# A weight's sign bit from a parametric relu on ScalarE instead of Abs and an instruction on VectorE

## The chip, the cores and the metric

One core of a Trainium2 chip runs the whole program. The metric is the device time of one launch in microseconds (us). Five engines work side by side, each with an in-order queue of its own: TensorE (PE; its weight loads are listed as PEld), VectorE (DVE), ScalarE (ACT), GpSimd (POOL) and SyncE (SP), which here issues all DMA transfers of tensors.

## The reference

An attention in two steps over 8 batches, 8 heads, 576 tokens and 64 features per head, followed by a Fourier mixing over tokens and features, a normalization without learned weights and a feed-forward part:

```
def sm_attn(qq, kk, vv):
    s = scale * np.matmul(qq, kk.transpose(0, 1, 3, 2))
    a = softmax(s)
    return np.matmul(a, vv)
p_packed = sm_attn(p, k, v)                 # 32 packed tokens per head
x = heads side by side of sm_attn(q, p_packed, p_packed)   # [8, 576, 512]
u = x + real(fft(fft(x, axis=1), axis=2))
un = (u - mean(u)) / sqrt(var(u) + 1e-6)
out = u + maximum(un @ w_ch1, 0) @ w_ch2    # w_ch1 [512, 2048], w_ch2 [2048, 512]
```

`w_ch1` and `w_ch2` come as 64-bit floats (a numpy scalar division made them so), everything else as 32-bit floats.

## The kernel before, in words

The 8 x 576 rows of `u` are worked in nine tiles of 512 rows. `front(b)` computes a batch's attention and Fourier mixing into rows of `u`; `ffn` runs the feed-forward part of one tile, and lets the `front` of the next batch advance a piece at a time in between. Only the front of batch 0 runs ahead of the first tile.

`ffn` goes over 16 blocks j of 128 hidden units. For each, `up(j)` (matmuls L648) multiplies the tile with a block of `w1` into PSUM tile `ph`, ScalarE takes the relu into `hh` (L654), VectorE subtracts that from the exact value into `hl` (L655), and `down(j - 1)` (matmuls L665) multiplies `hh` and `hl` of the block before with a block of `w2` into the accumulators `acc`. The PSUM tile `ph` is a single buffer, so the next `up` waits until `hl` has read it. To keep float32 accuracy each operand is split in two parts, and three matmuls are done for one. For the weights that split is `wsplits`: ScalarE rounds a block into `wr_h` (L99), GpSimd subtracts into `wr_l` (L100); it is done again in every tile, from `w1f` and `w2f`, which hold all weights in SBUF as 32-bit floats. At the end of a tile VectorE adds the result to `u` (L701), and a DMA writes it out.

The change is in `load_weights(j)`, which turns block j of both weights from 64-bit into 32-bit floats. This is done once, for 16 blocks x 2 weights = 32 blocks of 128 x 512. A 64-bit float is seen as two 32-bit words, `low` and `high`. Its fields are 1 sign bit, 11 exponent bits with a bias of 1023, 52 mantissa bits; a 32-bit float has 1, 8 (bias 127) and 23. The word `high` is read as if it were a 32-bit float: then the upper 8 of the 11 exponent bits stand in its exponent field. Multiplying by `REBIAS = 2.0 ** -112` takes 112 x 8 = 896 = 1023 - 127 off the 11-bit exponent. Abs clears the sign. Now a shift to the left by 3 (L179) puts exponent and 20 mantissa bits in place; L180 shifts the three missing mantissa bits in from `low`; L181 puts the sign bit back in from `high`. L179 to L181 are on VectorE, the Abs (L178) on ScalarE.

`fetch` (L166) brings a block of 64-bit words into a staging place, from SyncE's queue. The first six blocks go into parts of `w1f` and `w2f` that are not yet in use; from then on three places rotate, two buffers `wst` and one piece of `ubuf`. A fetch into a place waits until the last instruction that read it is done; before the change that is L181 of the block that stood there.

The order in which each engine works is set in two ways. From the second tile on it is the order of the program text (`manual_schedule`). Ahead of that, in the front of batch 0 and in all of the first tile, a planner lists the instructions of all engines by estimated costs and dependencies; all 32 blocks are converted in that part. Inside the first tile, the program text places `load_weights(j + 2)` in every second step, of which there are two in a block j.

Of the kernel before, what the change touches and what calls it, by code (L numbers as in the profile page):

```python
# [9 lines left out]
F32 = mybir.dt.float32  # L10
F32R = mybir.dt.float32r
I32 = mybir.dt.int32
AF = mybir.ActivationFunctionType
ALU = mybir.AluOpType
# [39 lines left out]
REBIAS = 2.0 ** -112  # L54
# [23 lines left out]
def tile_kernel(ctx, tc, kpT, qT, v, w1, w2, tabC, tabS, tabR, tabB, tabT, sel, ident_d, out):  # L78
    nc = tc.nc
# [78 lines left out]
    def fetch(j, n):  # L158
        i = stages.pop(0)
        if i is None:  # L160
            st = work.tile([P, 512, 2], I32, tag="wst", name="wst", bufs=2)
        elif i < 0:
            st = spot(n, i, [P, 512, 2]).bitcast(I32)
        else:
            st = ubuf[:, i:i + 2, :].rearrange("p a n -> p (a n)").bitcast(I32).rearrange("p (n t) -> p n t", t=2)
        nc.sync.dma_start(st, (w1, w2)[n][:, j, :].bitcast(I32).rearrange("p (n t) -> p n t", t=2))  # L166
        fetched[j, n] = st

    def load_weights(j):

        for n, dst in enumerate((w1f, w2f)):
            if (j, n) not in fetched:
                fetch(j, n)
            st = fetched.pop((j, n))
            low, high = st[:, :, 0], st[:, :, 1]
            c = dst[:, j, :].bitcast(I32)

            nc.scalar.activation(c.bitcast(F32), high.bitcast(F32), AF.Abs, scale=REBIAS)  # L178
            nc.vector.tensor_scalar(c, c, 3, None, ALU.logical_shift_left)  # L179
            nc.vector.scalar_tensor_tensor(c, low, 29, c, ALU.logical_shift_right, ALU.bitwise_or)  # L180
            nc.vector.scalar_tensor_tensor(c, high, -0x80000000, c,  # L181
                                           ALU.bitwise_and, ALU.bitwise_or)

# [540 lines left out]
    for j in range(ORDER[0].count("D"), LEAD):  # L726
        load_weights(j)
# [3 lines left out]
    for t, (first, tk) in enumerate(tiles):  # L731

        gen = front(t + 1) if t + 1 < B else iter(())
        ended = []

        def step(i):

            next_step()
            if t > 0 and i in (0, 2):
                next(rest, None)  # L740
            elif not ended and next(gen, None) == "rest":
                ended.append(gen)
            if t == 0 and i % 2 == 0 and i // 2 + LEAD < NJ:
                load_weights(i // 2 + LEAD)
            assert i < 2 * NJ - 1 or t + 1 >= B or ended

        nxt = Turned(tiles[t + 1][1]) if t + 1 < len(tiles) else None

        with tc.manual_schedule(engines=MANUAL) if t > 0 else nullcontext():
            ffn(first, cur, step, nxt, t + 1 >= B)  # L750
        cur, rest = nxt, gen
# [101 lines left out]
```

## Time and profile before

| | us |
|---|---|
| median of 3 runs (lowest to highest) | 1041.44 (1039.57 to 1041.57) |
| the profiled execution | 1041.16 |
| its span on the core | 1039.4 |

| engine | busy us | share of the span | instructions |
|---|---|---|---|
| PE | 981.9 | 94% | 5692 |
| DVE | 635.6 | 61% | 1296 |
| POOL | 470.1 | 45% | 419 |
| ACT | 425.7 | 41% | 883 |

The span is the time from the first to the last instruction on the core; some 1.8 us of the execution lie around it. A busy share is a mean over the whole span. The page also cuts the span into 40 slices of 26 us, and a table of stretches gives each engine's busy time between any two points of time.

### The profile page before, as it was taken

How to read it: one execution, taken by the hardware profiler on the slowest of the kernel's cores; microseconds unless marked ns; L12 is line 12 of the kernel's file. 1: busy time of each engine (PE TensorE's matmuls, PEld its weight loads, DVE VectorE, ACT ScalarE, POOL GpSimd, SP SyncE). 2: the span in 40 equal slices, each digit the busy share in tenths (PEclk: the TensorE clock that was granted, in tenths of full speed). 3: DMA queues.
4: the chain of work that ended last, by engine and by line, in shares of the span. 5: the costliest groups of instructions: out<-in, count | busy, mean ns of one | idle time of the engine just before them, and what ended most of it. 6: DMA issues, size and time to landing. Idle time of an engine off the chain costs nothing.

```text
span 1039.4 us, 14908 instructions
## 1 busy us (share of the span) xinstructions
PE 981.9 (94%) x5692; PEld 797.1 (77%) x5692; DVE 635.6 (61%) x1296; ACT 425.7 (41%) x883; POOL 470.1 (45%) x419
## 2 busy tenths in 40 slices
PE   6378879999999999999999999999999999999998
PEld 2356658778888788778877887788778888887886
DVE  3898999558655775569465946685658663114112
ACT  2554435344444344444344344344444443323222
POOL 1535544445444543454336534553445444444443
PEclk9699889999999999999999999999999999999999
DMA  9215425130004100310022002200120001001001
GB/s 336 94 57 188 149 81 143 40 118 28 1 1 138 49 1 1 134 52 1 2 92 94 1 1 91 96 1 1 41 97 1 1 2 40 1 1 42 1 1 41
DMA packets 17742, 58.64 MB, mean 56 GB/s; under 512 B 2081, under 2 KB 2465, under 8 KB 17670
## 3 DMA queue, kind: packets, MB, share of 16 engines
q1 hardware_dynamic: 17670, 57.68, 16.4%
q8 instruction: 45, 0.74, 0.3%
q14 instruction: 27, 0.22, 0.1%
HBM read 48.24 MB, written 9.44 MB: 55 GB/s over the span
## 4 chain that ended last, share of the span: by engine, by line
PE 74%; DVE 16%; ACT 4%; issue 3%; DMA 2%; POOL 2%; SPq 0%; ACTq 0%; DVEq 0%; POOLq 0%
PE ph L648 33%; PE acc L665 30%; DVE ubuf L568 2%; DVE turned L420 1%; PE po L327 1%; DVE w1f L181 1%; DVE w2f L180 1%; DVE hl L655 1%; DMA wst<-w 1%; ACT hh L654 1%; DVE turned L416 1%; ACT junk L218 1%; DVE w2f L181 1%; PE s L270 1%; DVE w1f L180 1%
## 5 line engine op out<-in xcount | busy, mean ns | idle before, releaser
L100 POOL TENSOR_TENSOR wr_l<-w1f,wr_h 128x512 fp32r<-128x512 f32 x144 | 192.3, 1335 | 402.4 <-ACT wr_h L99 402.4
L655 DVE SCALAR_TENSOR_TENSOR hl<-ph,hh 128x512 fp32r<-128x512 f32 x144 | 98.8, 686 | 297.9 <-ACT hh L654 297.8
L648 PE MATMUL ph<-uh,wr_h 128*128 128x512 f32 (+1 forms) x580 | 232.7, 401 | 16.4 <-DVE hl L655 14.5
L100 POOL TENSOR_TENSOR wr_l<-w2f,wr_h 128x512 fp32r<-128x512 f32 x144 | 195.1, 1355 | 90.0 <-ACT wr_h L99 88.6
L665 PE MATMUL acc<-wr_h,hh 128*128 128x512 f32 x576 | 228.0, 396 | 3.3 <-ACT wr_h L99 3.3
L648 PE MATMUL ph<-ul,wr_h 128*128 128x512 f32 (+1 forms) x580 | 230.0, 397 | 0.6 <-DVE ul L100 0.4
L648 PE MATMUL ph<-uh,wr_l 128*128 128x512 f32 (+1 forms) x580 | 230.2, 397 | 0.0
L665 PE MATMUL acc<-wr_l,hh 128*128 128x512 f32 x576 | 227.2, 394 | 3.1 <-POOL wr_l L100 3.1
L665 PE MATMUL acc<-wr_h,hl 128*128 128x512 f32 x576 | 226.1, 393 | 0.0
L654 ACT ACTIVATE hh<-ph 128x512 fp32r<-128x512 f32 x144 | 86.0, 597 | 285.3 <-PE ph L648 285.2
L648 PEld LDWEIGHTS ph<-uh,wr_h 128*128 128x128 f32 x580 | 110.3, 190 | 51.5 <-DVE hl L655 17.9
L648 PEld LDWEIGHTS ph<-uh,wr_l 128*128 128x128 f32 x580 | 110.4, 190 | 25.8 <-issue 1.7
L665 PEld LDWEIGHTS acc<-wr_h,hh 128*128 128x128 f32 x576 | 108.4, 188 | 27.3 <-ACT wr_h L99 3.5
L665 PEld LDWEIGHTS acc<-wr_l,hh 128*128 128x128 f32 x576 | 108.3, 188 | 26.7 <-POOL wr_l L100 5.5
L648 PEld LDWEIGHTS ph<-ul,wr_h 128*128 128x128 f32 x580 | 110.6, 191 | 23.3 <-DVE stat L214 1.1
L665 PEld LDWEIGHTS acc<-wr_h,hl 128*128 128x128 f32 x576 | 108.1, 188 | 23.2
L99 ACT CAST wr_h<-w1f 128x512 fp32r<-128x512 f32 x144 | 88.4, 614 | 11.6 <-DVE w1f L181 6.0
L99 ACT CAST wr_h<-w2f 128x512 fp32r<-128x512 f32 x144 | 89.4, 621 | 8.4 <-PE ph L648 6.9
L218 ACT ACTIVATE junk<-ubuf,stat 128x512 f32<-128x512 f32 x36 | 25.8, 717 | 69.4 <-DVE stat L214 69.4
L609 PE MATMUL untp<-ident,un 128*128 128x128 f32 x144 | 36.9, 272 | 1.6 <-DVE un L602 1.6
L238 PE MATMUL py<-gh,fh 128*128 128x258 f32 x64 | 19.0, 302 | 18.2 <-ACT fh L480 16.6
L100 POOL TENSOR_TENSOR gl<-turned,gh 128x516 fp32r<-128x516 f32 x16 | 24.5, 1532 | 23.4 <-ACT gh L99 22.4
(205 smaller groups left out, 1343.7 us busy)
## 6 DMA issues: line engine op xcount, KB each, us to landing
kp<-kpT SPq DMA_DIRECT2D x16, 608.0 KB, 4.9
out<-ubuf SPq DMA_DIRECT2D x36, 256.0 KB, 2.1
vt<-v SPq DMA_DIRECT2D x14, 640.0 KB, 4.6
wst<-w SPq DMA_DIRECT2D x17, 512.0 KB, 3.7
qt<-qT SPq DMA_DIRECT2D x14, 576.0 KB, 4.6
ubuf<-w SPq DMA_DIRECT2D x9, 512.0 KB, 3.7
w1f<-w SPq DMA_DIRECT2D x3, 512.0 KB, 10.9
w2f<-w SPq DMA_DIRECT2D x3, 512.0 KB, 11.3
```

The source lines that it names most:

```text
L99: nc.scalar.copy(hi, src)
L100: (lo_eng or nc.vector).tensor_tensor(lo, src, hi.bitcast(F32), ALU.subtract)
L180: nc.vector.scalar_tensor_tensor(c, low, 29, c, ALU.logical_shift_right, ALU.bitwise_or)
L181: nc.vector.scalar_tensor_tensor(c, high, -0x80000000, c, ALU.bitwise_and, ALU.bitwise_or)
L218: nc.scalar.activation(junk, u, AF.Square, bias=st[:, 1:2], scale=-1.0, accum_out=st[:, 2:3])
L238: nc.tensor.matmul(o, lh, rh, start=first, stop=False)
L568: nc.vector.scalar_tensor_tensor(u_of[key], qe, sign, pe, ALU.mult, ALU.add, accum_out=stat_of[key][:, 0:1])
L609: nc.tensor.transpose(tp[:, c * P:(c + 1) * P], un[:, c * P:(c + 1) * P], ident)
L648: nc.tensor.matmul(ph[:, t], l[:, c * P:(c + 1) * P], r[:, c, t], start=(k == 0), stop=(k == 11))
L654: nc.scalar.activation(hh[:, :T], ph[:, :T], AF.Relu)
L655: nc.vector.scalar_tensor_tensor(hl[:, :T], ph[:, :T], 0.0, hh[:, :T].bitcast(F32), ALU.max, ALU.subtract)
L665: nc.tensor.matmul(acc[i], l[:, w], r, start=(j == 0 and k == 0), stop=(j == NJ - 1 and k == 2))
```

## The change

ScalarE's Abs is replaced by a parametric relu with the same scale and `alpha = -2.0 ** 32`. A positive value comes out multiplied by 2^-112, as before. A negative one is also multiplied by -2^32: it becomes positive, and its exponent field is 32 larger, that is, bit 28 of the word is set (the rebiased exponent of these weights leaves that bit 0). The shift by 3 that follows takes bit 28 to bit 31, which is the sign bit. L181 is dropped.

```
-            nc.scalar.activation(c.bitcast(F32), high.bitcast(F32), AF.Abs, scale=REBIAS)
+            nc.scalar.activation(c.bitcast(F32), high.bitcast(F32), AF.Prelu, scale=REBIAS, alpha=-2.0 ** 32)
             nc.vector.tensor_scalar(c, c, 3, None, ALU.logical_shift_left)
             nc.vector.scalar_tensor_tensor(c, low, 29, c, ALU.logical_shift_right, ALU.bitwise_or)
-            nc.vector.scalar_tensor_tensor(c, high, -0x80000000, c,
-                                           ALU.bitwise_and, ALU.bitwise_or)
```

With a blank line that the diff adds, the parametric relu is L179 in the changed file, the shift L180 and the instruction with `low` L181; every later line has a number smaller by one (`hl` L654, the last addition L700).

## Rows read from the trace of the kernel before

**Rows 1.** The page, busy times and slices, whole span

```profile
PE 981.9 (94%) x5692; PEld 797.1 (77%) x5692; DVE 635.6 (61%) x1296; ACT 425.7 (41%) x883; POOL 470.1 (45%) x419
...
PE   6378879999999999999999999999999999999998
...
DVE  3898999558655775569465946685658663114112
...
PEclk9699889999999999999999999999999999999999
```

**Rows 2.** Stretches: start:end, length, each engine's busy us, clock, DMA share, GB/s

```profile
69.88:186.45 116.57, 99.96 (x528) 76.33 (x528) 111.05 (x209) 53.73 (x109) 60.77 (x48) 0.91 0.43 131
...
201.00:305.30 104.30, 103.97 (x641) 85.91 (x641) 69.27 (x147) 43.57 (x94) 45.73 (x39) 1.00 0.14 47
```

**Rows 3.** Line L655 to 205 us, who waited for it: us, times

```profile
  PEld ph L648: 17.9, 9
  PE ph L648: 14.5, 8
```

**Rows 4.** Chain of waits in order of time: start, us, what

```profile
68.67 0.60 DVE w1f L181
69.28 0.60 DVE w2f L181
69.88 0.60 DVE hl L655
```

**Rows 5.** Waits of SyncE's DMA queue, 62 to 186.45 us: total, times, longest

```profile
SPq L166 <- DVE w1f L181: 50.7, 12, 9.4
SPq L166 <- DVE w2f L181: 40.6, 11, 8.5
```

**Rows 6.** Line L181, one form: min/median/max ns, first and last start

```profile
L181 DVE SCALAR_TENSOR_TENSOR w1f<-w1f x3: 676/676/681, 54.1 to 74.3; 128x512 int32<-128x512 int32 x3
```

**Rows 7.** Stretches, line L181 alone: VectorE's busy us

```profile
48.07:69.88 21.81, 2.63 (x4) 0.95 0.18 55
69.88:186.45 116.57, 26.89 (x28) 0.91 0.43 131
```

**Rows 8.** VectorE in order of time: start, us, line, operation

```profile
90.56 1.79 DVE L181 SCALAR_TENSOR_TENSOR w1f<-wst,w1f 128x512 int32<-128x512 int32 x1
92.28 1.80 DVE L180 SCALAR_TENSOR_TENSOR w2f<-wst,w2f 128x512 int32<-128x512 int32 x1
```

**Rows 9.** GpSimd in order of time, the same stretch

```profile
90.34 1.47 POOL L100 TENSOR_TENSOR wr_l<-w1f,wr_h 128x512 fp32r<-128x512 f32 x1
91.76 1.77 POOL L100 TENSOR_TENSOR wr_l<-w2f,wr_h 128x512 fp32r<-128x512 f32 x1
```

**Rows 10.** Stretches, matmuls of L648 alone: TensorE's busy us, weight loads

```profile
69.88:186.45 116.57, 45.90 (x156) 32.18 (x156) 0.91 0.43 131
...
201.00:305.30 104.30, 47.67 (x192) 35.48 (x192) 1.00 0.14 47
```

**Rows 11.** Line L178, slowest form (ns) and ScalarE's idle time before it

```profile
L178 ACT ACTIVATE w1f<-w1f x3: 654/687/692, 23.2 to 48.1; 128x512 f32<-128x512 f32 x3
...
  DMA ubuf<-w: 14.5, 7
  DMA wst<-w: 12.4, 6
```

**Rows 12.** Line L179, VectorE's idle time before it: us, times

```profile
  ACT w2f L178: 2.0, 2
  ACT w1f L178: 1.7, 2
```

**Rows 13.** ScalarE's groups, whole span: the table load

```profile
L113 ACT ACT_TABLE_LOAD x1 | 1.3, 1283 | 0.7 <-PEq L845 0.7
```

**Rows 14.** ScalarE in order of time: Exp (L385), then Abs (L178)

```profile
109.33 0.69 ACT L385 ACTIVATE s<-s 128x576 f32<-128x576 f32 x1 [0.64 <-POOL s L382]
...
110.64 0.67 ACT L178 ACTIVATE w2f<-wst 128x512 f32<-128x512 f32 x1
```

## The prediction, made before the changed kernel ran

> **What bounds the kernel now.** I read the page's busy shares and slices first. TensorE is busy 94% of the span, and from the seventh of its 40 slices (156 us) on it shows nines; the slices ahead of that are the only ones in which it has gaps, in which VectorE shows eights and nines, and in which the granted clock shows a six and eights [rows 1]. The changed lines run only there, because the weights are rebuilt once, before and during the first tile of the feed-forward part, and are then kept.
>
> The table of stretches makes this a number. From 69.88 us (the first `hl` done) to 186.45 us (the last rebuilt weight done) VectorE is busy 111.05 of 116.57 us, so idle 5.5 us; TensorE is busy 99.96 and idle 16.6, at a mean granted clock of 0.91, a mixture of the two levels, 2.4 and 1.2 GHz. In a later stretch of 104.30 us TensorE is busy 103.97 at clock 1.00, the upper level throughout, and VectorE only 69.27 [rows 2]. So the first tile is limited by VectorE, the others by TensorE.
>
> Who waits for whom confirms it: TensorE's first matmuls of an `up` step wait for `hl`, VectorE's split of the hidden layer, eight times for 14.5 us, its weight loads 17.9 us [rows 3]. `hl` is short, but stands in VectorE's queue behind weight instructions: in the chain of waits it comes right after two L181 of 0.60 us each [rows 4]. Last, the DMA queue: the fetches of further weights wait 50.7 + 40.6 = 91.3 us, 23 times, and always for L181, which is the last reader of the staging buffer [rows 5]. VectorE therefore sets both TensorE's pace and the pace of the loads.
>
> **The change part by part.** *Removed: 32 times L181.* Alone it takes about 0.68 us [rows 6], but consecutive VectorE instructions overlap, and the chain shows a step of 0.60 [rows 4]. That is the lower bound of what leaves the queue: 32 x 0.60 = 19.2 us. The upper bound is their whole busy time, 2.63 + 26.89 = 29.5 us [rows 7], less the 0.07 of overlap each (0.68 - 0.60; 2.2 us): 27.3 us. The 8.1 us between the bounds are L181 instructions that ran longer, up to 1.79 us. These stretches coincide with GpSimd's `wr_l`: the L181 at 90.56 ran 1.79 us while GpSimd's subtraction ran from 90.34 to 91.81, and the L180 that follows ran 1.80 us beside the next one [rows 8, 9]. GpSimd's work stays, so part of this waiting goes to whatever VectorE does next. I take half of it: 19.2 + 4.05 = 23.3 us out of VectorE's queue.
>
> The Trainium skill bears on that half and speaks against it. Its page "SBUF — State Buffer" (section "SBUF: two separate sides") says that a VectorE instruction with two SBUF inputs and a GpSimd instruction that reads SBUF exclude each other for a whole instruction, the later one blocking. The trace agrees at 90.56 (GpSimd ends at 91.81, L181 0.54 us later). By the rule the wait would pass whole to the next L180, and the sum would be by the lower bound, 19.2.
>
> *What VectorE's relief is worth.* Of the 32, four lie before 69.88, on the chain there, 2.4 us by 0.60 each. The other 28 give 20.9 of the 23.3 us, so VectorE alone would finish the stretch in 116.57 - 20.9 = 95.7 us. What is late next is TensorE. Its 99.96 us contain matmuls at the low clock: L648 takes 45.90/156 = 0.294 us a piece here, 47.67/192 = 0.248 later, so 156 x 0.046 = 7.2 us go if the clock recovers with the gaps [rows 10]; TensorE's floor is 99.96 - 7.2 = 92.8 us. 95.7 stands above the floor by only 2.9, over 13 `up` steps of unequal VectorE load: where a step has little VectorE work, TensorE limits it and the saving is lost. For this I take off 3.3 us, a little over that margin, as an estimate. Gain: 23.3 - 3.3 = 20.0 us. The ends of this term: no loss (gain 23.3), or the largest gain, by the floor, 116.57 - 92.8 = 23.8 and 2.4 ahead of it, 26.2.
>
> *Buffers.* The staging buffer is now free after L180, an instruction earlier; each of the 23 waits of the fetches [rows 5] ends earlier. It is the same relief as above, and no second gain; it keeps the loads ahead.
>
> *Changed: Abs becomes Prelu, 32 times on ScalarE.* The trace of before has no Prelu. Abs takes 0.687 us in its slowest form, with waits of 26.9 us in 13 cases for the weight's DMA [rows 11]. ScalarE is busy in under half of the stretch, 53.73 of 116.57 [rows 2], and VectorE waits for it only four times, 3.7 us [rows 12]. So I take 0. Bounds: nothing gained below 0, since the instruction still reads and writes 128x512; above, one more instruction of the same kind each, 32 x 0.69 = 22 us of ScalarE time, hidden in its 62.8 idle us unless it comes while VectorE waits (four times: 2.8 us).
>
> *Moved.* Nothing in the source; but the first tile's order is not written by hand, the planner orders it over all engines and will do so anew with 32 instructions fewer. The trace can't price that; I widen the range by 3 us on both sides.
>
> *Sum.* The profiled execution took 1041.16 us (span 1039.4). 1041.2 - 20.0 = 1021.2. It lies 0.3 us under the median of the runs, which I neglect: 1021 us. All later tiles only start earlier.
>
> **The rivals.** *The loads bound the stretch.* Then only what is ahead of the stream goes: the seven L181 up to the one that the first of these fetches waits for, 7 x 0.60 = 4.2 us: 1037 us. For it: ScalarE already waits for DMA 13 times [rows 11]. Against: every fetch waits for L181, not for a DMA [rows 5].
>
> *Prelu needs another activation table than Exp.* The trace has one table load, 1.283 us [rows 13]. In ScalarE's order weights and Exp alternate (as at 109.33 and 110.64, [rows 14]) so that 12 loads would come: six into and six out of the weights' function. 12 x 1.28 = 15.4 us, if all on the path: 1021 + 15 = 1036 us. For it: nothing. Against: Abs, Copy, Square and Relu ran beside Exp on that one load. The Trainium skill, "ScalarE: Activation LUTs" (section "Table sets: the hidden batching unit"), names relu and abs among the fillers of Exp's set and does not name Prelu; its switch costs 2.66 us with the drain, by which the sum would be 1021 + 32 = 1053, and the trace shows no drain's price.
>
> *Slower: VectorE runs into its own data.* VectorE's queue is in order. If it reaches L179 before the weight has landed, `hl` waits behind it. Today ScalarE waits 26.9 us for weights and VectorE feels 3.7 of it, being late itself [rows 11, 12]. If all of it came through, 26.9 - 3.7 = 23.2 us: 1021 + 23 = 1044 us. It decides the sign from 20 us on, 0.87 us for each of the 23 streamed weights. Against: a faster VectorE frees the buffers sooner, so the loads start sooner too.
>
> **How the numbers follow.** Forecast 0.77; loads 0.09; table 0.04; slower by VectorE's own data or by a bad new order 0.07; a gain wholly lost in between 0.03. The forecast's own range: 26.2 + 3 gained at the most (1012), 19.2 - 3.3 - 3 at the least (1028), and 2.8 more if Prelu is dear (1031). To leave out no more than 2 in 10 I reach part of the way to the two cases at 1036 and 1037: 1012 to 1033. A run of this kernel can tell about 0.2%, 2.1 us, from no change. Faster: 0.77 + 0.09 + 0.04 = 0.90, less 0.01 for the tails; same 0.04; slower 0.07.
>
> **What would show it.** Right: L181's group gone, VectorE's busy time in the first 190 us down by 20 to 27 us, the first L701 at about 181 instead of 201 us, `up` steps (one `hl` to the next) about 7.4 instead of 9.0 us, TensorE's wait for `hl` cut to a few us, the clock near 1.00, the tiles after it unchanged in length. L180 longer than before would show that the waiting for GpSimd passed on. Wrong: more than one table load; VectorE's idle time before L179 in tens of us; ScalarE's instruction of L178 well over 0.69 us; or a first tile as long as before with TensorE's gaps put down to something else, `wr_h` or the DMA.

## The result and the profile after

The changed kernel takes 1026.9 us in the median (4 runs, 1025.99 to 1027.88) against 1040.56 (4 runs) for the kernel before beside it; the ratio is 0.9876, 95% interval [0.9861, 0.9891]. It is 13.7 us faster; forecast were 20.0, range 1012 to 1033.

The page of the changed kernel, busy times and slices, to be set beside [rows 1]:

```profile
span 1025.3 us, 14876 instructions
...
PE 978.5 (95%) x5692; PEld 795.6 (78%) x5692; DVE 608.8 (59%) x1264; ACT 425.0 (41%) x883; POOL 463.1 (45%) x419
...
PE   6489889999999999999999999999999999999998
...
DVE  3897994559465856677556846594658562114112
...
PEclk9699899999999999999999999999999999999999
```

VectorE has 32 instructions and 26.8 us less to do. ScalarE's busy time is the same within 0.7 us. Where the 14 us come from is seen by cutting the span at the first addition into `u` (L701 before, L700 after), that is, at the end of the first tile. First the kernel before, then the changed one (columns as in [rows 2]):

```profile
0.00:201.10 201.10, 152.75 (x921) 114.58 (x922) 165.75 (x335) 89.73 (x186) 88.64 (x101) 0.91 0.42 135
201.10:1039.40 838.30, 829.17 (x4772) 682.54 (x4771) 469.83 (x963) 335.94 (x697) 381.43 (x319) 1.00 0.11 37
```

```profile
0.00:187.22 187.22, 149.40 (x921) 113.13 (x922) 139.58 (x302) 89.29 (x186) 83.36 (x101) 0.91 0.43 146
187.22:1025.30 838.08, 829.15 (x4772) 682.50 (x4771) 469.26 (x963) 335.69 (x697) 379.70 (x319) 1.00 0.11 37
```

The eight later tiles take 838.3 and 838.1 us: all of the gain, 13.9 us, lies in the first tile and ahead of it. VectorE was relieved of 26.2 us there, and half of that arrived. I cut the first tile at three instructions: the first, sixth and twelfth `hl` and the end. The kernel before, then the changed one:

```profile
69.80:114.86 45.06, 38.49 (x240) 27.48 (x241) 41.25 (x69) 19.93 (x42) 23.32 (x17) 0.89 0.54 172
114.86:170.64 55.78, 47.48 (x225) 37.70 (x224) 54.17 (x112) 25.39 (x51) 27.78 (x22) 0.91 0.36 107
170.64:201.09 30.45, 27.98 (x135) 22.52 (x135) 20.70 (x40) 13.41 (x27) 15.89 (x13) 1.00 0.17 51
```

```profile
66.95:103.91 36.96, 35.77 (x240) 25.89 (x241) 29.29 (x58) 21.10 (x43) 20.97 (x17) 0.95 0.69 232
103.91:159.97 56.06, 46.79 (x227) 37.60 (x227) 51.76 (x109) 26.23 (x51) 26.65 (x23) 0.91 0.38 119
159.97:187.22 27.25, 27.11 (x133) 22.10 (x132) 11.04 (x22) 11.93 (x25) 14.63 (x14) 1.00 0.00 1
```

Ahead of the first `hl` 2.85 us are gained, in the first stretch 8.1, in the last 3.2; the middle one, the longest, takes 0.3 us longer than before. In the first and the last TensorE is now busy nearly throughout (35.77 of 36.96, 27.11 of 27.25), so relieving VectorE further can bring little there. In the middle VectorE is nearly as full as before, 51.76 of 56.06, and TensorE idles 9.3 us. Yet it is in the middle that the change took VectorE instructions away too. What took their place is told by the order: between the sixth and the twelfth `hl` the kernel before has finished 10 conversions of 32 (the 18th to the 27th), the changed one 13 (the 20th to the 32nd, all that are left). The planner moved conversions, and three short instructions that prepare the next tile, forward into the time that the change made free; little is left for VectorE in the last stretch (11.04 of 27.25).

The lines that answer to [rows 3], [rows 5], [rows 11] and [rows 12], from the changed kernel. Who waited for `hl`, line L654, to 190 us:

```profile
  PEld ph L647: 9.8, 4
  PE ph L647: 9.6, 3
```

What the fetches on SyncE's queue waited for:

```profile
SPq L166 <- DVE w1f L181: 32.5, 12, 12.4
SPq L166 <- DVE w2f L181: 32.2, 11, 8.1
```

The parametric relu, line L179, the form that was slowest before:

```profile
L179 ACT ACTIVATE w1f<-w1f x3: 652/681/687, 22.5 to 47.2; 128x512 f32<-128x512 f32 x3
```

VectorE's idle time before the shift, line L180, and ScalarE's table load:

```profile
  ACT w2f L179: 4.3, 5
  ACT w1f L179: 2.7, 5
```

```profile
L113 ACT ACT_TABLE_LOAD x1 | 1.3, 1283 | 0.7 <-PEq L844 0.7
```

TensorE still waits 9.6 us for `hl`, in only three waits. The longest, 4.40 us, ends at 116.15. ScalarE's half of that step, `hh`, was done at 112.00, but `hl` stood in VectorE's queue behind three conversion instructions and two short transposes (start, us, instruction):

```profile
110.24 1.65 DVE L181 SCALAR_TENSOR_TENSOR w2f<-wst,w2f 128x512 int32<-128x512 int32 x1
111.81 1.49 DVE L180 TENSOR_SCALAR w1f<-w1f 128x512 int32<-128x512 int32 x1
113.23 1.48 DVE L180 TENSOR_SCALAR w2f<-w2f 128x512 int32<-128x512 int32 x1
...
115.45 0.64 DVE L654 SCALAR_TENSOR_TENSOR hl<-ph,hh 128x512 fp32r<-128x512 f32 x1
```

Each of the two shifts took some 1.5 us there, against 0.43 in the median; GpSimd was at work beside them, from 111.30 to 114.42.

The parametric relu takes what Abs took, on the same one table load.

### The profile page after: what moved, and what is told of

Its sections match the earlier page's. It is cut to its first block, busy times and chain, and to the rows that moved or that the text cites. A ratio compares the mean times of both kernels' runs of the same rounds, so it can differ in the third digit from the quotient of the medians.

```text
span 1025.3 us, 14876 instructions
## 1 busy us (share of the span) xinstructions
PE 978.5 (95%) x5692; PEld 795.6 (78%) x5692; DVE 608.8 (59%) x1264; ACT 425.0 (41%) x883; POOL 463.1 (45%) x419
## 4 chain that ended last, share of the span: by engine, by line
PE 76%; DVE 11%; ACT 5%; DMA 3%; issue 2%; POOL 2%; ACTq 0%; SPq 0%; DVEq 0%; POOLq 0%
PE ph L647 35%; PE acc L664 30%; DVE ubuf L567 2%; DMA wst<-w 2%; DVE turned L419 1%; ACT hh L653 1%; PE po L326 1%; PE s L269 1%; ACT junk L217 1%; DVE turned L415 1%; POOL wr_l L100 1%; PE e1tp L303 1%; DVE hl L654 1%; ACT wr_h L99 1%; DVE w2f L181 1%
## 5 line engine op out<-in xcount | busy, mean ns | idle before, releaser
L654 DVE SCALAR_TENSOR_TENSOR hl<-ph,hh 128x512 fp32r<-128x512 f32 x144 | 98.8, 686 | 305.3 <-ACT hh L653 305.0
L100 POOL TENSOR_TENSOR wr_l<-w2f,wr_h 128x512 fp32r<-128x512 f32 x144 | 192.4, 1336 | 91.9 <-ACT wr_h L99 91.9
L664 PEld LDWEIGHTS acc<-wr_l,hh 128*128 128x128 f32 x576 | 108.2, 188 | 26.8 <-POOL wr_l L100 5.4
L567 DVE SCALAR_TENSOR_TENSOR ubuf<-qe,pe 128x512 f32<-128x512 f32 x32 | 34.6, 1115 | 0.5
```

What stands on the lines that cost most here:

```text
L100: (lo_eng or nc.vector).tensor_tensor(lo, src, hi.bitcast(F32), ALU.subtract)
L567: nc.vector.scalar_tensor_tensor(u_of[key], qe, sign, pe, ALU.mult, ALU.add, accum_out=stat_of[key][:, 0:1])
L654: nc.vector.scalar_tensor_tensor(hl[:, :T], ph[:, :T], 0.0, hh[:, :T].bitcast(F32), ALU.max, ALU.subtract)
L664: nc.tensor.matmul(acc[i], l[:, w], r, start=(j == 0 and k == 0), stop=(j == NJ - 1 and k == 2))
```

## The experiments

Times are medians; beside each stands the ratio to the kernel before, run beside it on the same chip.

**Which of the two edits it is.** e1 is the changed kernel with Abs back, e2 the kernel before with the parametric relu:

```
e1  -  AF.Prelu, scale=REBIAS, alpha=-2.0 ** 32      +  AF.Abs, scale=REBIAS
e2  -  AF.Abs, scale=REBIAS                          +  AF.Prelu, scale=REBIAS, alpha=-2.0 ** 32
```

> The changed kernel with Abs put back in place of the parametric relu, the VectorE instruction still dropped; the weights lose their sign, so that part of the computation is wrong. Every engine has the same instruction order as the changed kernel. Theory (the gain is VectorE's relief, the kind of activation costs nothing): within 1.5 us of the changed kernel's 1026.9. Rival (the parametric relu itself is slower or faster than Abs on the path): off by more than 3 us, 32 instructions by 0.1 us or more.

> The kernel before with the parametric relu in place of Abs, and the VectorE instruction kept (it sets a sign bit that is already set). Instruction order as in the kernel before. Theory: within 1.5 us of the kernel before, 1040.6, for it is the VectorE instruction that counts. Rival (parametric relu matters): off by more than 3 us.

e1: 1027.67 us, 0.9884 [0.9869, 0.9899]; e2: 1039.35 us, 0.9998 [0.9985, 1.0011]. The whole gain is the dropped VectorE instruction's; the kind of activation costs nothing, and the rival of a dear or cheap parametric relu falls. In the first tile e2 has the instruction order of before and e1 that of the changed kernel, so their traces also repeat the cut of the first tile. The middle stretch of e2 and of e1:

```profile
113.92:169.28 55.36, 45.83 (x220) 36.22 (x221) 53.98 (x111) 24.73 (x49) 27.56 (x22) 0.94 0.36 108
```

```profile
103.50:159.81 56.31, 46.27 (x225) 36.92 (x226) 52.15 (x108) 25.96 (x51) 25.93 (x23) 0.94 0.38 119
```

Again the middle is no shorter with the instruction dropped.

**Is it VectorE's relief, or the luck of a new order?** In e3 (changed) and e4 (before) the compute engines follow the program text in the first tile too:

```
-        with tc.manual_schedule(engines=MANUAL) if t > 0 else nullcontext():
+        with tc.manual_schedule(engines=MANUAL):
```

> The changed kernel with the first tile's compute engines in the order of the program text instead of the planner's, so that two weights are converted for each hl and none ahead of need. Theory A (VectorE's relief was spent by the planner on conversions far ahead of need, and hl and with it TensorE came late): faster than the changed kernel, 1014 to 1022 us. Theory B (what limits the changed kernel's first tile is the arrival of the weights): no faster, 1027 us or more, with VectorE idle before the shift for the conversion's activation well above the 7.0 us of the changed kernel.

> The kernel before with the first tile in the order of the program text. Theory A: VectorE is full in nearly all steps there, in any order, so little moves: 1033 to 1042 us, and the distance to the changed kernel in the same order is larger than 13.7 us, 16 to 24. Rival D (the gain of the change was the luck of a new planner's order, not VectorE's relief): the two kernels in the order of the text lie within 6 us of each other.

e3: 1035.39 us, 0.9959 [0.9943, 0.9975]; e4: 1050.56 us, 1.0105 [1.0089, 1.0121]. With the first tile in the order of the text (the front of batch 0 ahead of it is still the planner's) the change is worth 15.2 us, so luck (rival D) falls. All three numbers of theory A missed, the 15.2 too, for which it said 16 to 24: the order of the text makes the changed kernel 8.5 us slower and the kernel before 10.5. It does bring two conversions for each `hl`, but TensorE's order is fixed with it, and it stands for 7.7 us in front of the front's matmuls, in e3 (`who waited <- for whom: total, times, longest`):

```profile
PE py L237 <- ACT fh L479: 7.7, 1, 7.7
```

So e3 says nothing on theory A; it needs an order changed in one place. The time fits theory B, but B's sign is missing: VectorE's idle time before the shift is 8.2 us, hardly more than the 7.0 of the changed kernel.

**Conversions held back.** One ordering edge on VectorE, in e5 for all blocks with k = 2, in e6 with k = 3:

```
-            nc.vector.tensor_scalar(c, c, 3, None, ALU.logical_shift_left)
+            sh = nc.vector.tensor_scalar(c, c, 3, None, ALU.logical_shift_left)
+            if j - k in hl_of:          # hl_of[j]: the hl of block j
+                tc.add_manual_dep(sh.ins, hl_of[j - k], NoSync, ...)
```

> The changed kernel with one ordering edge added on VectorE: the shift of block j's weights stands behind hl of block j - 2, so that conversions can't run further ahead of need than two blocks; the planner orders all else. Theory A (in the changed kernel the planner spends VectorE's relief on conversions ahead of need, in the middle of the first tile, while TensorE waits for hl): 1017 to 1024 us. Rival A2 (in the middle it is the front's own work that fills VectorE, the conversions are not what holds hl up): 1025 us or more, with TensorE's wait for hl as long as in the changed kernel, 9.6 us.

> The same with the edge to hl of block j - 3, one block looser. Theory A: between the changed kernel (1026.9) and the tighter edge, 1019 to 1026 us. Rival A2: within 1.5 us of the changed kernel.

e5: 1025.21 us, 0.9852 [0.983, 0.9873]; e6: 1027.69 us, 0.9878 [0.9857, 0.99]. In the medians e5 is 1.7 us faster than the changed kernel, and 1.2 outside theory A's range; the intervals of the two ratios overlap. e6 is no faster. Held back from the start, the conversions leave the first stretch, where there is room, for the middle and the last. 12 still lie in the middle, against 13, but they are spaced: two for each `hl`, where the changed kernel has 1, 3, 1, 0, 5 and 3. And the middle of e5 is 4.2 us shorter than the changed kernel's:

```profile
105.55:157.39 51.84, 43.39 (x222) 34.90 (x221) 47.46 (x106) 26.87 (x52) 25.80 (x23) 0.97 0.45 135
```

So in the middle the edge did in part what theory A said: TensorE waits 6.2 us for `hl` there instead of 8.1 (A2 said as long as before). The larger part is that its own work takes 43.39 us instead of 46.79, with 222 matmuls instead of 227 and at clock 0.97 instead of 0.91. In the total little of it shows, for in this execution the first `hl` came only at 70.39 us. In the changed kernel it came at 66.95 and in e1 at 66.04, although the compute engines have the same order in all three up to there; why is open. The 2.85 us that I counted ahead of the first `hl` are smaller than this difference between single traces, so they are not shown to come from the change.

**The price of one VectorE instruction in every conversion.** e7 drops the instruction with `low` as well, e8 does the sign instruction of the kernel before twice:

```
e7  -            nc.vector.scalar_tensor_tensor(c, low, 29, c, ALU.logical_shift_right, ALU.bitwise_or)
e8  +            nc.vector.scalar_tensor_tensor(c, high, -0x80000000, c,
    +                                           ALU.bitwise_and, ALU.bitwise_or)
```

> The changed kernel without the VectorE instruction that puts the three lowest mantissa bits in either, so 32 instructions of the same kind fewer again; the weights lose their last three bits. If VectorE still limits the middle of the first tile: 5 to 10 us faster than the changed kernel, 1017 to 1022 us, less than the first 32 gave since TensorE has only some 11 idle us left there. If the arrival of the weights is the limit (theory B): less than 3 us faster.

> The kernel before with the sign instruction done twice, 32 VectorE instructions more. If VectorE limits the whole first tile before the change, each costs its full place in the queue, 0.60 to 0.85 us: 1060 to 1067 us, and so the gain of the change was less than the price because something else took over after it. If one such instruction is worth 0.43 us in general (13.7 / 32, the planner fitting the rest into gaps): 1054 us.

e7: 1022.76 us, 0.9827 [0.9804, 0.985]; e8: 1054.03 us, 1.0135 [1.0106, 1.0163]. From four VectorE instructions a conversion to one, the steps in the medians are 13.1, 13.7 and 4.1 us, where 32 instructions of at least 0.60 us are 19.2. So even from e8 to the kernel before, with VectorE fuller still, only 0.41 us each arrive, which is what the second of e8's two views said. e7's 4.1 us lie between the 5 to 10 that I expected and the 3 of theory B. The two kernels were not timed side by side, and by the ratios to the kernel before the step is 5.1, so the time alone doesn't decide between the two. The trace does: all weights are converted by 112.1 us, so from there on their arrival can't be the limit. e7's three stretches:

```profile
69.98:103.75 33.77, 33.75 (x240) 25.60 (x241) 19.26 (x48) 22.90 (x47) 16.84 (x15) 1.00 0.87 293
103.75:154.22 50.47, 43.02 (x219) 34.49 (x218) 38.05 (x87) 19.93 (x41) 24.21 (x23) 0.97 0.11 35
154.22:183.01 28.79, 28.79 (x142) 23.83 (x141) 9.90 (x23) 12.14 (x25) 14.73 (x14) 1.00 0.00 1
```

In the first stretch TensorE has no gap left (33.75 of 33.77). In the middle only three conversions are left, VectorE idles 12.4 us, and the stretch still takes 50.5 us. The 5.6 us gained there are partly lost again: the first `hl` comes 3.0 us later than in the changed kernel, and the last stretch is 1.5 us longer. The chain of waits shows what the middle consists of (start, us, what):

```profile
112.98 0.69 DVE hl L653
113.67 0.64 DVE s L373
114.33 0.76 DVE m L379
115.12 1.87 DVE s L380
117.01 0.70 ACT s L383
117.73 0.70 ACT s L384
118.45 0.76 DVE z L392
119.23 1.09 DVE d L393
120.35 0.62 DVE z L394
120.97 0.66 DVE s L396
121.63 0.18 DVE z L395
121.81 0.54 DVE hl L653
```

It is the second softmax of the next batch's front, step after step; `hl` stands at its end in VectorE's queue, and TensorE waited 2.94 us for this one (at 122.40).

**Conversions out of the middle.** From this came theory M and its rival W. e9 has the edge of e5 for blocks 9 to 15 alone (`if j >= 9 and j - 2 in hl_of`); e10 has no edge but one piece of that front on GpSimd (`ES` has an entry for batch 0, batch 1 and the rest; 1 is GpSimd); e11 has both; e12 is e9 from block 8 on:

```
-ES = (1, 0, 0)
+ES = (1, 1, 0)
```

> The changed kernel with the ordering edge (shift of block j behind hl of block j - 2) for blocks 9 to 15 alone: eight conversions instead of thirteen lie between the sixth and the twelfth hl, the others go behind it, where VectorE idles. Theory M (in the middle of the first tile VectorE is full, with conversions and with the next front's work together, and hl waits; the ends are TensorE's): five conversions of some 1.1 us out of the middle, 1020 to 1024 us. Rival W (there the front is a chain of dependent steps that holds hl up whatever else VectorE has to do): within 2 us of the changed kernel, 1025 to 1029.

> The changed kernel with one piece of the front of batch 1, 24 short instructions for the edges of the folded rows (some 5 us in all), on GpSimd instead of VectorE; the conversions as in the changed kernel. Theory M: about 4 us come out of the full middle, 1021 to 1024 us. Rival W: the chain gets no shorter, GpSimd being slower at each of them: 1026 us or more.

> Both edits together. Theory M: 1017 to 1022 us, the sixth to the twelfth hl in 47 to 51 us instead of 56.1, TensorE's wait for hl under 4 us. Rival W: 1025 us or more.

> As the edge from block 9 on, but from block 8 on, so that two more conversions leave the stretch before the sixth hl for the middle; timed in five rounds to see whether the faster version is reproduced by a neighbour. If the middle is held up by the front's own chain once VectorE has slack there: the middle again at 51 to 53 us, and 1022 to 1025 us in all. If VectorE's load alone set the middle: two conversions more cost some 2 us, 1025 to 1027.

| | us | ratio to before |
|---|---|---|
| e9 | 1023.51 | 0.9844 [0.9825, 0.9863] |
| e10 | 1029.03 | 0.9900 [0.9880, 0.9920] |
| e11 | 1025.06 | 0.9863 [0.9840, 0.9885] |
| e12 | 1024.12 | 0.9845 [0.9826, 0.9865] |

The middle stretch of e9, e10, e11 and e12, in this order:

```profile
103.18:155.54 52.36, 44.90 (x221) 36.00 (x221) 42.46 (x97) 23.67 (x47) 25.21 (x23) 0.93 0.30 101
```

```profile
103.94:160.13 56.19, 45.49 (x220) 36.56 (x219) 47.98 (x84) 26.09 (x51) 33.44 (x47) 0.88 0.38 119
```

```profile
103.61:155.88 52.27, 44.84 (x219) 35.42 (x218) 39.99 (x73) 23.71 (x47) 30.59 (x47) 0.93 0.32 101
```

```profile
106.14:156.43 50.29, 43.12 (x218) 34.10 (x217) 44.12 (x101) 23.68 (x47) 23.64 (x23) 0.97 0.37 118
```

e9 takes 9.3 us of VectorE's work out of the middle (51.76 to 42.46) and shortens it by 3.7, half of it in TensorE's gaps (9.3 to 7.5 us) and half in TensorE's own work (46.79 to 44.90). Its 1023.51 us lie in theory M's range. 1.3 of the 3.7 come back in its last stretch, where TensorE is busy throughout and now has 140 matmuls instead of 133:

```profile
155.54:184.11 28.57, 28.57 (x140) 23.58 (x140) 18.85 (x34) 14.63 (x29) 15.61 (x14) 1.00 0.19 56
```

But e9 does two things: eight conversions lie in the middle instead of thirteen, and they are spaced. e5, with twelve spaced, shortens the middle as much. What is shown is that conversions right in front of `hl` cost time, as at 116.15 in the changed kernel; that fewer of them help as such is not.

e10 takes 3.8 us out of the middle by way of GpSimd and shortens nothing (56.19), as W said. It is no clean test of VectorE's load, for it makes the front's chain longer. In VectorE's queue an instruction of that chain now waits 2.94 us for GpSimd's pieces, `hl` stands behind it, and the second long wait of TensorE grows from 3.7 to 6.0 us:

```profile
133.35 0.46 DVE L437 TENSOR_TENSOR eo<-a 128x287 f32<-128x287 f32 x1 [2.94 <-POOL f L468]
```

In e11 both numbers of M miss (1017 to 1022 us, and under 4 us of waiting for `hl`, which is 7.7): 2.5 us less for VectorE than in e9 shorten the middle by 0.1, and in all e11 is 1.6 us slower than e9. e12 leaves 1.7 us more work in the middle than e9, and its middle is 2.1 us shorter; in all it is no faster, for in its trace the first `hl` comes 2.3 us later. So load alone does not set the middle: it takes 50 to 52 us in e5, e7, e9, e11 and e12, with VectorE busy between 38 and 47 us of it. e9 and e12 agree within 0.6 us. Of the kernels that do the whole computation they are the fastest: all runs of e9 (1022.62 to 1024.20) lie below all of the changed kernel (1025.99 to 1027.88). The two were not timed side by side, though, and the intervals of their ratios to the kernel before just overlap.

## Why the prediction was right in direction and too large in size

- *What bounds the kernel*: right. The gain is VectorE's relief in the first tile (e1, e2), and the later tiles take as long as before. One reading on the way was wrong: VectorE shows eights and nines in later slices too [rows 1], but TensorE has no gaps there.
- *Out of VectorE's queue, 23.3 us*: too small. In the first tile VectorE's busy time, in which overlapping instructions count once, fell by 26.2 us (165.75 to 139.58). L181's own 29.5 us [rows 7] overlap with its neighbours by 4.1 us, not by 2.2: worked out from the starts and durations of before, the busy time of the first tile without L181 is 140.34 us, 25.4 less. Of the waiting for GpSimd, which I put at 8.1 us, I let half go on to other instructions; on balance none did. The sign that I had named for it is missing too. The instruction with `low`, 32 times, before and after:

```profile
0.00:201.10 201.10, 27.86 (x32) 0.91 0.42 135
```

```profile
0.00:187.22 187.22, 26.46 (x32) 0.91 0.43 146
```

  The Trainium skill's rule ("SBUF — State Buffer", "SBUF: two separate sides") fits single instructions of before; that it would hand all of the waiting on, as I read it, does not agree with these numbers. That fewer VectorE instructions meet GpSimd's less often would explain it; it was not tested.
- *3.3 us taken off where TensorE is the limit*: this is the term that was badly mis-sized. It measured 26.2 - 13.9 = 12.3 us, and so much longer VectorE now idles in the first tile: 6.5 us more in the last stretch and 3.9 in the first, where TensorE is busy nearly throughout, 2.7 more in the middle, and 0.7 less ahead of the first `hl`. That the time still came within 6 us of the forecast owes something to luck, for the relief was taken too small as well. My sum ended with the last rebuilt weight and took what follows as fixed. Cut there, the first tile reads so, before and after:

```profile
69.80:186.45 116.65, 99.96 (x528) 76.33 (x528) 111.13 (x210) 53.81 (x109) 60.77 (x48) 0.91 0.43 131
186.45:201.09 14.64, 13.98 (x69) 11.38 (x70) 4.99 (x8) 4.93 (x9) 6.22 (x5) 1.00 0.00 0
```

```profile
66.95:155.58 88.63, 78.17 (x443) 59.69 (x444) 77.32 (x154) 45.99 (x90) 46.20 (x38) 0.92 0.53 172
155.58:187.22 31.64, 31.50 (x156) 25.89 (x155) 14.77 (x35) 13.27 (x28) 16.05 (x15) 1.00 0.00 1
```

  The stretch shrank by 28.0 us, more than I said, but in it TensorE did 78.17 us of work instead of 99.96: 11 `hl` are done at its end instead of 13, and 31.6 us follow instead of 14.6, with TensorE full. In my sum the relief was spread over 13 steps; the planner spent it on finishing the conversions two steps sooner. By e9 some 3.4 us of it come back when the order is changed. For the rest, TensorE is close to its limit in the first and the last stretch; that the front's chain holds `hl` up in the middle is read from e7's chain and from a middle that stays at 50 to 52 us, and no experiment singles it out.
- *TensorE's floor*: its form was right, its place wrong. I took one floor for the whole stretch, 92.8 us; in truth TensorE is nearly at its work in the first and the last part and 9.3 us above it in the middle. So "a few us" of waiting for `hl` were 9.6, the clock in the middle stayed at 0.91 instead of near 1.00, and the steps were 7.4 us only up to the sixth `hl`, 9.3 from there to the twelfth.
- *Prelu for 0 us, one table load*: right (0.681 against 0.687 us; 1283 ns once).
- *The loads* as a bound: no. The fetches still wait for VectorE, 64.7 instead of 91.3 us. *VectorE running into its own data*: the mechanism is there, its idle time before the shift rose from 3.7 to 7.0 us in ten waits, but it is far from the 20 us at which it would have decided the sign.

## What to carry to other kernels

When an overloaded engine is relieved, ask for each stretch which engine is next, and not only for the sum: one floor for the whole hid that half of the relief fell where another engine was already at its limit, or where a dependent chain in the same in-order queue sets the pace. Count what else is finished by the moment that your sum ends with; if a planner orders the work, it may have bought that moment with work that then comes later. And before a difference of 2 or 3 us between stretches of two traces is read as an effect, look at how far apart two traces of the same order lie.

## What the runs showed that I had not expected

One more or one fewer VectorE instruction in each conversion moved the time by nearly the same amount from four instructions to three and from three to two, 13.1 and 13.7 us, though the place in the queue alone is 19.2. That a planner which fills gaps gives back a constant part would explain it; no run shows it. And with short instructions moved to GpSimd the kernel was 2.1 us slower in the median (e10 against the changed kernel, intervals overlapping) although GpSimd was busy only 26.65 of 56.06 us there and VectorE was nearly full: the wait that this put into VectorE's queue counted for more than the work that it took out. What stays open is how much of the middle would go if the front's chain stood behind `hl` in VectorE's queue; that was not tried.
